# Two-term fp16 weights split from float32 in place, an output factor computed at a layer's start, and key norms by one squaring and one sum per half step

## The chip, the cores and the metric

The kernel runs on one core of a Trainium2 chip. A core has a matrix engine (TensorE, "PE" in the profile, with its weight loads as "PEld"), VectorE ("DVE"), ScalarE ("ACT"), GpSimd ("POOL"), SyncE ("SP", which issues the transfers here) and 16 DMA engines. Each engine takes its instructions strictly in order and waits on semaphores for the others. The metric is the device time of one execution in microseconds, the median of several.

## The reference

Delta-rule attention over 4 x 8 heads of 768 steps with head size 48, then two feed-forward layers over the 3072 tokens of width 384:

```python
k_n = k / (np.linalg.norm(k, axis=-1, keepdims=True) + 1e-06)
for t in range(S):
    kt, vt, bt = (k_n[:, :, t], v[:, :, t], beta[:, :, t, None])
    y[:, :, t] = np.einsum('bhd,bhde->bhe', q[:, :, t], state)
    v_old = np.einsum('bhde,bhd->bhe', state, kt)
    state = state + bt[:, :, :, None] * np.einsum('bhd,bhe->bhde', kt, vt - v_old)
...
h = x @ w_in          # first layer:  g = max(0.01 h, h)
g = ...               # second layer: g = h - tanh(h)
return g @ w_out      # d_model 384, d_ff 2048
```

All arrays are float32. The weights come in as 64-bit words (two 32-bit words for each number).

## The kernel before

**Numbers.** TensorE works on fp16. Each float32 operand is scaled by a power of two and split into a high fp16 part and a low one (value minus high part), and a product takes three matmuls: high by high, high by low, low by high.

**Work.** The 768 steps are cut into twelve chunks of 64 steps (n = 0 to 11), two to a unit u. For each chunk the attention makes normalised keys (`keys`, `key_scale`, `key_split`), Gram matrices (`grams`), products with q, states and outputs y (`outputs`). For each unit there is a triangular inverse (`inverses`): VectorE transposes `Gd` into `X`, GpSimd runs 30 steps of two tensor_tensor instructions each (`Gd<-X`, then `X<-X,Gd`), ScalarE and VectorE split the result (`Gd<-X`, `Gd<-X,Gd`), VectorE transposes it back, and merges on TensorE (`a_ps<-X,AT` and `a_ps<-XF,PM`) follow. y of a chunk is scaled and split by `to_xa` and `x_split` (ScalarE `xhi<-x,sxs`, then VectorE `x<-x,sxs,xhi`); that is the input of the first feed-forward layer.

**Layers.** `layer(n, i)` runs feed-forward layer i for chunk n, in the order (0,0), (1,0), (0,1), (1,1), (2,0) and so on: 24 passes, called pass 0 to pass 23 here. Each has eight parts p. `h_part` does 18 matmuls into `h_ps`, then ScalarE (and VectorE for i = 1) makes `sx`, and a high and a low `g`; `o_part` does the matmuls into the accumulators `o`, three parts behind. There is one pair of accumulators, so the first `o_part` of a pass waits until those of the pass before are copied out, for i = 1 by `osb<-o,kap` on ScalarE and on VectorE, one bank each.

**Weights.** Four weight tensors (0: w1_in in tile `wi_104`, 1: w1_out in `wo_106`, 2: w2_in in `wi_105`, 3: w2_out in `wo_107`) are loaded as word pairs. `w_f32` assembles float32 numbers in the destination itself with three VectorE instructions on 768 columns, ScalarE sums their squares, and `splits` turns each block of 384 columns into a high and a low fp16 half.

**Order.** The program runs a planner (`Plan`) while it is built: each instruction has an assumed cost, each engine an assumed clock, and side jobs (attention, weights) are put between the matmuls when they look ready. `tt` gives an elementwise instruction to VectorE or GpSimd, `cp` to VectorE or ScalarE, whichever the planner thinks ends first. All instructions of a scratch kind share one ring of four buffers (tag `sx`). A change of any instruction therefore reorders the program on every engine.

Nearly all instructions go through one line (L160), so the profile is read by tile names.

Of the kernel before, what the change touches and what calls it, by code (L numbers as in the profile page):

```python
# [191 lines left out]
def kernel(  # L192
# [18 lines left out]
    NG = 2  # L211
# [35 lines left out]
    def copy(o, i, scale=1.0):  # L247
        act.activation(out=o, in_=i, func=ACTF.Copy, scale=scale)
# [4 lines left out]
    def tt(o, a, b, op, lead=2.0):  # L253

        f = {e: plan.finish(e, "tensor_tensor", [a, b], [o]) for e in ("dve", "pool")}
        (dve if f["dve"] + lead < f["pool"] else pool).tensor_tensor(out=o, in0=a, in1=b, op=op)
# [85 lines left out]
    def at(*aps):  # L342
        return plan.at(*aps)
# [32 lines left out]
    class Weights:  # L376
# [36 lines left out]
            done.add((self.i, "s"))  # L413

        def splits(self):
            for f in range(NF):
                yield plan.t["act"]
                w = s_p.tile([128, DM], F32, tag="sx", name="wst")
                copy(w, self.f32[:, f], sw[:, self.i:self.i + 1])
                copy(self.dst[:, f, 0], w)  # L420
                tt(self.dst[:, f, 1], w, self.dst[:, f, 0], ALU.subtract, bias())
                done.add((self.i, f))

    def weights():
        wi = [words(w.rearrange("p f c n -> p (f c n)")) for w in WI2]
# [121 lines left out]
    def key_scale(a, y, t):  # L547

        dve.tensor_scalar(out=t, in0=a, scalar1=2.0 ** -100, scalar2=None, op0=ALU.max)
        dve.tensor_scalar(out=y.bitcast(I32), in0=t.bitcast(I32), scalar1=1, scalar2=POW2,  # L550
                          op0=ALU.logical_shift_right, op1=ALU.bitwise_and)
        dve.tensor_scalar(out=t, in0=y, scalar1=2.0 ** 64 / 0.85, scalar2=None, op0=ALU.mult)
        dve.reciprocal(out=y, in_=t)
        for it in range(5):
            if it in (1, 3):
                yield plan.t["dve"]
            dve.tensor_tensor(out=t, in0=y, in1=y, op=ALU.mult)
            dve.scalar_tensor_tensor(out=t, in0=t, scalar=-0.5, in1=a, op0=ALU.mult, op1=ALU.mult)
            dve.scalar_tensor_tensor(out=y, in0=t, scalar=1.5, in1=y, op0=ALU.add, op1=ALU.mult)
        dve.tensor_tensor(out=t, in0=a, in1=y, op=ALU.mult)  # L560
        dve.tensor_scalar(out=t, in0=t, scalar1=1e-6, scalar2=1.0 / KS, op0=ALU.add, op1=ALU.mult)
        dve.reciprocal(out=y, in_=t)
# [11 lines left out]
    def keys(n):  # L574

        yield from wait(("s", n - 4))
        load_k(n)
        kf = kf_t.pop(n)
        n2 = sm_p.tile([128, 3, NM], F32, tag="n2", name="n2", bufs=1)
        a, y, t = (n2[:, i] for i in range(3))  # L580
        for m in range(NM):
            if m % tune("k_m") == 0:
                yield max(plan.t["act"], at(kf))
            junk = s_p.tile([128, D], BF16, tag="junk", name="junk", bufs=1)
            square_sum(a[:, m:m + 1], kf[:, m], junk)
        yield max(plan.t["dve"], at(a))
        yield from key_scale(a, y, t)
        yield max(plan.t["act"], at(y))
        key_split(n, kf, y, tune("lead_k"))
# [376 lines left out]
    def h_part(i, x, p, kap):  # L966

        ps = ps_h.tile([128, 2 * N], F32, tag="h", name="h_ps")
        order = [(t, a, b) for t in range(KT) for a, b in ((0, 0), (0, 1), (1, 0))]
        if p == 0:  # L970
            order = [(t, a, 0) for t in range(KT) for a in range(2)] + [(t, 0, 1) for t in range(KT)]
        for j in range(2):
            for n, (t, a, b) in enumerate(order):
                mm(ps[:, j * N:(j + 1) * N], WI[i][:, 2 * p + j, a, t], x[b][:, t], n == 0, n == 3 * KT - 1)
                if n % tune("every") == tune("every") - 1:
                    side.step()
        sx = s_p.tile([128, 2 * N], F32, tag="sx", name="sx")
        if i == 0:
            act.activation(out=sx, in_=ps, func=ACTF.Prelu, scale=C0, alpha=0.01)
        else:  # L980
            act.activation(out=sx, in_=ps, func=ACTF.Tanh, scale=kap[:, 0:1])
            dve.scalar_tensor_tensor(out=sx, in0=sx, scalar=kap[:, 1:2], in1=ps, op0=ALU.mult, op1=ALU.add)
        g = g_p.tile([128, 2, 2 * N], F16, tag="g", name="g")
        if i == 0:
            copy(g[:, 0], sx)
            tt(g[:, 1], sx, g[:, 0], ALU.subtract, bias())
        else:
            split(g[:, 0], g[:, 1], sx, C0)
        return g

    def o_part(i, po, g, p):

        for j in range(2):
            f = 2 * p + j
            first, last = f == 0, f == NF - 1
            gj = g[:, :, j * N:(j + 1) * N]
            for o in range(KT if i == 0 else 2):
                if i == 0 and o == 0 and first:
                    mm(po[0], maskp[:, 0:1].to_broadcast([128, 128]), maskp[:, 0:1].to_broadcast([128, 512]), True, False)
                for n, (a, b) in enumerate(((0, 0), (0, 1), (1, 0))):  # L1000
                    if i == 0:
                        mm(po[o // 2][:, o % 2 * N:o % 2 * N + N], WO[0][:, f, a, o * 128:(o + 1) * 128], gj[:, b],
                           o == 2 and first and n == 0, o > 0 and last and n == 2)
                    else:
                        mm(po[o][:, 0:DM], gj[:, b, o * 128:(o + 1) * 128], WO[1][:, f, a], first and n == 0,
                           last and n == 2)
                side.step()

# [96 lines left out]
    def o_next():  # L1105
        n, i, p, g, kap, sx, po = pend.pop(0)
        if p == 0:
            po += [ps_o.tile([128, 512], F32, tag=f"o{o}", name=f"o{o}") for o in range(2)]
        need((2 * i + 1, 2 * p + 1))
        side.step(plan.at(g, WO[i][:, 2 * p], WO[i][:, 2 * p + 1]))  # L1110
        o_part(i, po, g, p)
        if p < NP - 1:
            return
        if i == 0:
            gen = to_xb(n, po, sx)
            e = side.add(gen, "xb")
            side.advance(e)
            return
        out_scale(kap)
        for o in range(2):  # L1120
            ob = s_p.tile([128, DM], F32, tag="sx", name="osb")
            if o % 2:
                dve.tensor_scalar(out=ob, in0=po[o][:, 0:DM], scalar1=kap[:, 2:3], scalar2=None, op0=ALU.mult)
            else:
                copy(ob, po[o][:, 0:DM], kap[:, 2:3])
            for h in range(2):
                r0 = (2 * o + h) * S + n * C
                sp.dma_start(out=out[r0:r0 + C], in_=ob[h * C:(h + 1) * C])

    def layer(n, i):  # L1130
# [8 lines left out]
        else:  # L1139
# [5 lines left out]
            x, sx = xb_t.pop(n)  # L1145
            need((2, "s"))
            kap = kappa(sx)
        po = []
        for p in range(NP):
            need((2 * i, 2 * p + 1))  # L1150
# [84 lines left out]
```

## Time and profile before

| what | value |
|---|---|
| median of 3 runs | 1221.16 us (1218.24 to 1222.01) |
| profiled execution | 1222.18 us, span 1220.3 us, mean granted clock 0.97 |
| TensorE busy | 1013.1 us, 83% of the span |
| VectorE, ScalarE, GpSimd busy | 736.5, 634.0 and 509.1 us |
| read from and written to memory | 41.09 MB and 4.72 MB |

Shares are over the whole span. A row of a timeline begins with its start in microseconds from the span's start and its length; a bracket at its end is the idle time of the engine ahead of it, and what ended that. A group row gives the count, the busy time, the mean of one in ns, and after the second bar the idle time ahead of them.

### The profile page before, as it was taken

The page shows a single profiled execution, that of the slowest core. Times are in us where ns is not written, and L with a number is a line of the kernel's source. Part 1 is how long each engine was busy: PE and PEld are TensorE (multiplying, and loading weights), DVE is VectorE, ACT ScalarE, POOL GpSimd, SP SyncE. Part 2 cuts the span into 40 slices and gives each one's busy share as a digit, 9 for nine tenths or more (in the row PEclk, how much of TensorE's full clock was granted, in tenths as well). Part 3 has the DMA queues.
Part 4 walks back from the last instruction along what each step waited for, and adds up shares of the span by engine and source line. Part 5 has one row for each costly group of instructions (what it writes and reads, how often), then busy time and mean ns, then how long its engine had stood idle before and what let it go on. Part 6 is the DMA issues. An engine that isn't in the chain of part 4 may idle for free.

```text
span 1220.3 us, 36850 instructions
## 1 busy us (share of the span) xinstructions
PE 1013.1 (83%) x16216; PEld 831.8 (68%) x16216; DVE 736.5 (60%) x1592; ACT 634.0 (52%) x1409; POOL 509.1 (42%) x635
## 2 busy tenths in 40 slices
PE   0301658898798989989999888899999999999998
PEld 0201547686686878857787766678867888778875
DVE  7997896857567567777755665546753064420243
ACT  3555679695356655645567534435543364333332
POOL 4597446388214872483332682485110321012100
PEclk9999999899898989989999898999999999999999
DMA  9423133100001000000111000001000000000001
GB/s 363 154 84 113 55 106 96 37 24 1 16 23 39 24 22 17 26 23 24 39 32 37 24 1 16 10 8 33 25 10 14 14 12 2 11 17 1 1 1 27
DMA packets 21857, 48.17 MB, mean 39 GB/s; under 512 B 4288, under 2 KB 7360, under 8 KB 21696
## 3 DMA queue, kind: packets, MB, share of 16 engines
q1 hardware_dynamic: 21696, 45.82, 11.9%
q8 instruction: 126, 2.06, 0.7%
q14 instruction: 35, 0.29, 0.1%
HBM read 41.09 MB, written 4.72 MB: 38 GB/s over the span
## 4 chain that ended last, share of the span: by engine, by line
PE 51%; DVE 26%; ACT 11%; POOL 8%; issue 4%; DMA 0%; ACTq 0%; SPq 0%; DVEq 0%; POOLq 0%
PE o L160 21%; PE h_ps L160 19%; PE a_ps L160 11%; DVE n L160 4%; POOL X L160 3%; POOL Gd L160 3%; DVE x L160 2%; ACT g L160 2%; DVE wi L160 2%; DVE g L160 2%; DVE sx L160 2%; DVE wo L160 2%; ACT junk L160 1%; ACT sx L160 1%; DVE X L160 1%
## 5 line engine op out<-in xcount | busy, mean ns | idle before, releaser
L160 PE MATMUL h_ps<-x,wi 128*128 128x256 f16 x3456 | 427.9, 276 | 18.3 <-DVE x L160 12.3
L160 PEld LDWEIGHTS <-wi 128*128 128x128 f16 x3456 | 336.5, 99 | 77.6 <-issue 23.6
L160 PE MATMUL o<-wo,g 128*128 128x384 f16 x1152 | 214.9, 337 | 25.5 <-ACT osb L160 16.0
L160 POOL TENSOR_TENSOR g<-sx,g 128x512 f16<-128x512 f32 x78 | 93.1, 1194 | 311.6 <-ACT g L160 291.6
L160 PE MATMUL o<-g,wo 128*128 128x256 f16 x1728 | 210.6, 275 | 0.0
L160 PEld LDWEIGHTS <-wo 128*128 128x128 f16 x1728 | 167.4, 98 | 32.3 <-issue 10.5
L160 ACT ACTIVATE g<-sx 128x512 f16<-128x512 f32 x192 | 121.0, 630 | 120.2 <-DVE sx L160 117.2
L160 PEld LDWEIGHTS <-g 128*128 128x128 f16 x1152 | 113.7, 100 | 96.0 <-issue 36.0
L160 DVE SCALAR_TENSOR_TENSOR sx<-sx,kap,h_ps 128x512 f32<-128x512 f32 x96 | 71.2, 741 | 92.9 <-ACT sx L160 92.6
L160 POOL TENSOR_TENSOR Gd<-X 128x30 f32<-128x30 f32 (+9 forms) x180 | 110.8, 616 | 33.3 <-DVE X L160 19.5
L160 POOL TENSOR_TENSOR X<-X,Gd 128x30 f32<-128x30 f32 (+9 forms) x180 | 114.8, 638 | 14.1
L160 DVE SCALAR_TENSOR_TENSOR g<-sx,g 128x512 f16<-128x512 f32 x96 | 74.3, 774 | 67.4 <-ACT g L160 67.4
L160 ACT ACTIVATE sx<-h_ps,kap 128x512 f32<-128x512 f32 x96 | 65.4, 681 | 81.6 <-PE h_ps L160 71.3
L160 ACT ACTIVATE sx<-h_ps 128x512 f32<-128x512 f32 x96 | 56.5, 589 | 93.9 <-PE h_ps L160 87.6
L160 PEld LDWEIGHTS <-KTp 64*64 64x64 f16 x3360 | 66.2, 118 | 36.4 <-issue 34.4
L160 POOL TENSOR_TENSOR P<-P,maskp 128x1024 f16<-128x1024 f16 x24 | 52.6, 2196 | 61.4 <-DVE P L160 58.2
L160 PE MATMUL a_ps<-ab,ones 128*128 128x1 bf16 x124 | 11.7, 168 | 75.3 <-DVE ab L160 73.4
L160 PEld LDWEIGHTS <-KN 64*64 64x64 f16 x1824 | 37.5, 120 | 39.7 <-issue 35.7
L160 PE MATMUL a_ps<-Q,Sb 128*128 128x64 f16 x528 | 35.7, 199 | 13.2 <-DVE Sb L160 13.2
L160 PEld LDWEIGHTS <-ones 128*128 128x128 bf16 x124 | 7.8, 102 | 54.0 <-DVE ab L160 50.0
L160 PE MATMUL a_ps<-Q,KTp 64*64 64x64 f16 x1152 | 25.4, 201 | 23.1 <-ACT Q L160 20.2
L160 ACT ACTIVATE x<-a_ps,qs 32x128 f32<-32x128 f32 (+1 forms) x57 | 25.5, 447 | 31.4 <-PE a_ps L160 28.2
(161 smaller groups left out, 1533.1 us busy)
## 6 DMA issues: line engine op xcount, KB each, us to landing
wo<-in_w_in_dram SPq DMA_DIRECT2D x32, 384.0 KB, 6.1
qf<-in_q_dram SPq DMA_DIRECT2D x24, 256.0 KB, 2.6
wi<-in_w_out_dram SPq DMA_DIRECT2D x14, 384.0 KB, 7.8
kf<-in_k_dram SPq DMA_DIRECT2D x12, 384.0 KB, 4.1
vf<-in_v_dram SPq DMA_DIRECT2D x12, 384.0 KB, 4.1
out_dram<-osb SPq DMA_DIRECT2D x48, 96.0 KB, 2.2
wo<-in_w_out_dram SPq DMA_DIRECT2D x8, 384.0 KB, 3.8
stage<-in_w_out_dram SPq DMA_DIRECT2D x8, 384.0 KB, 3.8
```

What stands on the lines that cost most here:

```text
L160: return getattr(self.eng[eng], op)(*args, **kw)
```

## The change

Three edits, and what the planner makes of them.

`splits` takes two blocks at a time. ScalarE writes the scaled fp16 high half of 768 columns into a scratch tile `wh`, VectorE writes the low half from the float32 numbers over their own place (`lo_of`), and a transfer on SyncE's queue copies `wh` into the other half. The halves of a weight change places, hence `1 - a` where they are read. In `keys`, eight heads are squared at once and VectorE sums them; in `key_scale` an integer first guess and three refinements stand in place of a reciprocal and five. `out_scale`, three small VectorE instructions, goes from the end of a pass with i = 1 to its start.

```diff
         def splits(self):
-            for f in range(NF):
+            s_ = sw[:, self.i:self.i + 1]
+            for f in range(0, NF, 2):
                 yield plan.t["act"]
-                w = s_p.tile([128, DM], F32, tag="sx", name="wst")
-                copy(w, self.f32[:, f], sw[:, self.i:self.i + 1])
-                copy(self.dst[:, f, 0], w)
-                tt(self.dst[:, f, 1], w, self.dst[:, f, 0], ALU.subtract, bias())
-                done.add((self.i, f))
+                w = s_p.tile([128, 2, DM], F16, tag="sx", name="wh")
+                copy(w, self.f32[:, f:f + 2], s_)
+                lo_of(self.dst[:, f:f + 2, 0], self.f32[:, f:f + 2], s_, w)
+                sp.dma_start(out=self.dst[:, f:f + 2, 1], in_=w)
+                done.update((self.i, f + i) for i in range(2))
...
     def key_scale(a, y, t):
-        dve.tensor_scalar(out=y.bitcast(I32), in0=t.bitcast(I32), scalar1=1, scalar2=POW2,
-                          op0=ALU.logical_shift_right, op1=ALU.bitwise_and)
-        dve.tensor_scalar(out=t, in0=y, scalar1=2.0 ** 64 / 0.85, scalar2=None, op0=ALU.mult)
-        dve.reciprocal(out=y, in_=t)
-        for it in range(5):
-            if it in (1, 3):
+        dve.tensor_scalar(out=t.bitcast(I32), in0=t.bitcast(I32), scalar1=1, scalar2=None,
+                          op0=ALU.logical_shift_right)
+        dve.tensor_scalar(out=y.bitcast(I32), in0=t.bitcast(I32), scalar1=-1.0, scalar2=float(0x5F375A00),
+                          op0=ALU.mult, op1=ALU.add)
+        for it in range(3):
+            if it == 1:
...
-        for m in range(NM):
-            if m % tune("k_m") == 0:
-                yield max(plan.t["act"], at(kf))
-            junk = s_p.tile([128, D], BF16, tag="junk", name="junk", bufs=1)
-            square_sum(a[:, m:m + 1], kf[:, m], junk)
+        for g in range(NG):
+            gs = slice(g * GM, (g + 1) * GM)
+            yield max(plan.t["act"], at(kf))
+            qs = s_p.tile([128, GM, D], F32, tag="sx", name="ksq")
+            act.activation(out=qs, in_=kf[:, gs], func=ACTF.Square)
+            dve.tensor_reduce(out=a[:, gs], in_=qs, axis=AX.X, op=ALU.add)
...
-        out_scale(kap)
         for o in range(2):
             ob = s_p.tile([128, DM], F32, tag="sx", name="osb")
...
             need((2, "s"))
             kap = kappa(sx)
+            out_scale(kap)
```

Over the whole program VectorE goes from 1593 to 1547 instructions, ScalarE from 1157 to 923 activations, GpSimd from 639 to 594, SyncE's transfers rise by 32, and TensorE keeps its 16216 matmuls.

On GpSimd, inside the first inverse (steps 15 and 16 of its 30), the difference reads:

```order
 L160 TENSOR_TENSOR Gd<-X 128x16x15
 L160 TENSOR_TENSOR X<-X,Gd 128x16x15
-L160 TENSOR_TENSOR wi_104<-wst,wi_104 128x384
 L160 TENSOR_TENSOR Gd<-X 128x15x16
 L160 TENSOR_TENSOR X<-X,Gd 128x15x16
```

Four such splits of w1_in stood among the steps of the first inverse, and none stands there now; the second inverse had six of w2_out and has none.

On VectorE, behind the input of pass 0 (`x<-x,sxs,xhi` is the low half of that input), what follows before is the last of the word assembly (from `stage`) and attention work:

```order
L160 SCALAR_TENSOR_TENSOR x<-x,sxs,xhi 128x768
L160 COPY x<-xhi 128x768
L160 SCALAR_TENSOR_TENSOR wo_107<-stage,wo_107 128x768
L160 SCALAR_TENSOR_TENSOR Gd<-a_ps,maskb,Gd 128x256
L160 SCALAR_TENSOR_TENSOR AT<-a_ps,half,AT 128x256
```

In the changed program the assembly of w2_out only begins there, among the splits of w2_in and the norms of keys (`n_1757`):

```order
L160 SCALAR_TENSOR_TENSOR wo_107<-wo_107 128x768
L160 TENSOR_SCALAR wo_107<-wo_107 128x768
L160 SCALAR_TENSOR_TENSOR wo_107<-wo_107 128x768 x2
L160 SCALAR_TENSOR_TENSOR wi_105<-wi_105,sw,wh 128x2x384
L160 TENSOR_TENSOR n_1757<-n_1757 128x16
L160 SCALAR_TENSOR_TENSOR n_1757<-n_1757 128x16 x2
```

Between the low half of pass 0's input and that of pass 1's stand 88 instructions before and 140 now. The 52 more are 9 scalar_tensor_tensor and 5 tensor_scalar of word assembly, 8 splits, 17 small key instructions, 3 sums, 3 key scalings, 3 key splits, a transpose of `Gd` and some ten instructions on one column, less some copies.

At the first end of a pass with i = 1 VectorE had, before:

```order
L160 SCALAR_TENSOR_TENSOR g<-sx,g 128x512
L160 TENSOR_SCALAR kap<-sw 128x1
L160 RECIPROCAL kap<-kap 128x1
L160 TENSOR_TENSOR kap<-kap 128x1
L160 TENSOR_SCALAR osb<-o_4335,kap 128x384
```

and now:

```order
L160 SCALAR_TENSOR_TENSOR sx<-sx,kap,h_ps 128x512
L160 SCALAR_TENSOR_TENSOR g<-sx,g 128x512
L160 TENSOR_SCALAR osb<-o_4348,kap 128x384
L160 SCALAR_TENSOR_TENSOR x<-x,sxs,xhi 128x768
L160 COPY x<-xhi 128x768
```

The three instructions on `kap` are gone from that place; they follow the six of `kappa` at the pass's start.

## Rows read from the trace of the kernel before

**Rows 1.** The page: busy time by engine.

```profile
PE 1013.1 (83%) x16216; PEld 831.8 (68%) x16216; DVE 736.5 (60%) x1592; ACT 634.0 (52%) x1409; POOL 509.1 (42%) x635
```

**Rows 2.** Windows: length, then busy PE, PEld, DVE, ACT, POOL; clock, DMA share, GB/s.

```profile
113.00:181.70 68.70, 35.97 (x1138) 34.05 (x1138) 64.10 (x110) 49.63 (x116) 32.50 (x29) 1.00 0.31 105
181.70:235.00 53.30, 43.81 (x598) 37.13 (x598) 40.65 (x89) 42.54 (x104) 25.61 (x23) 0.97 0.24 75
235.00:381.40 146.40, 133.82 (x2313) 107.14 (x2313) 92.34 (x214) 88.37 (x217) 71.39 (x98) 0.93 0.07 19
381.40:943.00 561.60, 515.56 (x9125) 420.77 (x9125) 356.60 (x816) 291.91 (x677) 261.45 (x349) 0.96 0.08 22
943.00:1220.30 277.30, 270.55 (x2641) 220.71 (x2638) 89.51 (x199) 107.35 (x179) 40.03 (x33) 1.00 0.04 9
```

**Rows 3.** Chain of waits, first inverse's first and last step; GpSimd's group of splits, 50 to 110.

```profile
50.00 0.85 POOL Gd L160
...
109.68 0.33 POOL X L160
...
L160 POOL TENSOR_TENSOR wi<-wst,wi 128x384 f16<-128x384 f32 x4 | 5.3, 1332 | 0.0
```

**Rows 4.** VectorE's timeline: split of the first inverse, inputs of pass 0 and pass 1.

```profile
111.41 1.54 DVE L160 TENSOR_TENSOR Gd<-X,Gd 128x1024 f16<-128x1024 f32 x1 [4.91 <-ACT Gd L160]
...
179.65 1.01 DVE L160 SCALAR_TENSOR_TENSOR x<-x,sxs,xhi 128x768 f16<-128x768 f32 x1
...
233.54 1.01 DVE L160 SCALAR_TENSOR_TENSOR x<-x,sxs,xhi 128x768 f16<-128x768 f32 x1
```

**Rows 5.** TensorE's timeline: first matmuls of pass 0 and of pass 1.

```profile
181.70 5.79 PE L160 MATMUL h_ps<-x,wi 128*128 128x256 f16 x27 [5.57 <-DVE x L160]
...
235.00 2.50 PE L160 MATMUL h_ps<-x,wi 128*128 128x256 f16 x11 [3.86 <-DVE x L160]
```

**Rows 6.** VectorE's groups: two of word assembly (the second from 181.7 to 235), key instructions.

```profile
L160 DVE SCALAR_TENSOR_TENSOR wi<-wo,wi 128x768 int32<-128x768 int32 x32 | 34.3, 1071 | 0.7
...
L160 DVE SCALAR_TENSOR_TENSOR wo<-stage,wo 128x768 int32<-128x768 int32 x7 | 11.5, 1642 | 0.2
...
L160 DVE SCALAR_TENSOR_TENSOR n<-n 128x16 f32<-128x16 f32 x100 | 30.7, 307 | 3.4
```

**Rows 7.** ScalarE's groups: key squares, their accumulator reads, high half of x.

```profile
L160 ACT ACTIVATE junk<-kf 128x48 bf16<-128x48 f32 x160 | 37.9, 237 | 2.7
L160 ACT ACTIVATION_READ_ACCUMULATOR junk<-kf 128x1 f32 x160 | 30.1, 188 | 0.0
L160 ACT ACTIVATE xhi<-x,sxs 128x768 f16<-128x768 f32 x24 | 22.2, 924 | 4.9 <-DVE sxs L160 3.0 <-DVE ab L160 1.7 <-DVE n L160 0.2
```

**Rows 8.** GpSimd's timeline, second inverse: first and last instruction, one split; two GpSimd groups.

```profile
261.45 0.25 POOL L160 TENSOR_TENSOR Gd<-X 128x30 f32<-128x30 f32 x1 [1.07 <-DVE X L160]
264.39 0.91 POOL L160 TENSOR_TENSOR wo<-wst,wo 128x384 f16<-128x384 f32 x1
313.61 0.64 POOL L160 TENSOR_SCALAR X<-bt 128x32 f32<-128x32 f32 x1
...
L160 POOL TENSOR_TENSOR g<-sx,g 128x512 f16<-128x512 f32 x78 | 93.1, 1194 | 311.6 <-ACT g L160 291.6 <-issue 17.6 <-DVE p L160 1.3
L160 POOL TENSOR_TENSOR P<-P,maskp 128x1024 f16<-128x1024 f16 x24 | 52.6, 2196 | 61.4 <-DVE P L160 58.2 <-DVE n L160 1.9 <-DVE p L160 1.3
```

**Rows 9.** TensorE's waits from 235 on: in total, times, longest; the end of pass 2.

```profile
PE o L160 <- ACT osb L160: 19.6, 8, 5.9
...
325.41 0.58 ACT L160 ACTIVATE osb<-o,kap 128x384 f32<-128x384 f32 x1 [1.28 <-DVE kap L160]
326.05 0.65 PE L160 MATMUL o<-wo,g 128*128 128x384 f16 x3 [4.15 <-ACT osb L160]
```

**Rows 10.** One kind of transfer: count, size of one, median us from issue to landing.

```profile
qf<-in_q_dram SPq DMA_DIRECT2D x24, 256.0 KB, 2.6
```

More of the change, by code (lines that the diff above doesn't have):

```diff
@@ L973, in h_part @@
             for n, (t, a, b) in enumerate(order):
-                mm(ps[:, j * N:(j + 1) * N], WI[i][:, 2 * p + j, a, t], x[b][:, t], n == 0, n == 3 * KT - 1)
+                mm(ps[:, j * N:(j + 1) * N], WI[i][:, 2 * p + j, 1 - a, t], x[b][:, t], n == 0, n == 3 * KT - 1)
                 if n % tune("every") == tune("every") - 1:
@@ L1001, in o_part @@
                     if i == 0:
-                        mm(po[o // 2][:, o % 2 * N:o % 2 * N + N], WO[0][:, f, a, o * 128:(o + 1) * 128], gj[:, b],
+                        mm(po[o // 2][:, o % 2 * N:o % 2 * N + N], WO[0][:, f, 1 - a, o * 128:(o + 1) * 128], gj[:, b],
                            o == 2 and first and n == 0, o > 0 and last and n == 2)
                     else:
-                        mm(po[o][:, 0:DM], gj[:, b, o * 128:(o + 1) * 128], WO[1][:, f, a], first and n == 0,
+                        mm(po[o][:, 0:DM], gj[:, b, o * 128:(o + 1) * 128], WO[1][:, f, 1 - a], first and n == 0,
                            last and n == 2)
```

## The prediction

> **What bounds the kernel now.** I read the page first, for the busy times [rows 1]: TensorE is busy for 83% of the span, so 207 us of it are gaps, and the question is where they lie. The windows answer that [rows 2]. From 943 us to the end TensorE is busy for 270.55 of 277.3 us. From 381 to 943 it is busy for 92%, from 235 to 381 for 91%, from 181.7 to 235 for 82%, and ahead of 181.7 hardly at all. So the first 235 us hold most of what can be won, and work taken from the other engines after 943 us is worth nothing.
>
> The chain of waits shows who holds the start: from 50.00 to 110.01 us it runs through GpSimd, from the first to the last step of the first triangular inverse [rows 3]. Then VectorE takes over. It splits the inverse at 111.41 and writes the last input of pass 0 at 179.65 [rows 4], and in the window from 113 to 181.7, nearly the same stretch, it is busy for 64.10 of 68.70 us [rows 2]. TensorE starts pass 0 at 181.70 and pass 1 at 235.00, both times after an idle stretch that ended with VectorE's `x`, of 5.57 and 3.86 us [rows 5]. In the 53.3 us between, TensorE has 43.81 us of work and VectorE 40.65 [rows 2]. From 235 on TensorE's largest wait that the change touches is for `osb`, 19.6 us in 8 places [rows 9].
>
> The profiled execution took 1222.18 us, 1.0 above the median shown. The sum is made against it, and the median's worth is taken off at the end. A measurement of this kernel can tell 0.3%, 3.7 us, from no change.
>
> **The first inverse: -0.9 and -6.2 us.** (a) Seven of `key_scale`'s small VectorE instructions go, at 307 ns [rows 6] 2.1 us. A product that now stands on VectorE and a sum take about half of it back, so GpSimd starts the inverse some 0.9 earlier (bounds 0 and -2.1). (b) Four splits of w1_in leave the inverse itself, 5.3 us of the 60.0 [rows 3]. It ends near 103.8 instead of 110.01 if nothing takes their place. The cost of a lesser gain is the rival on contention, below.
>
> **VectorE from the inverse to pass 0: -5.9 us.** (c) In the order, the work between the split of the inverse and the last input of pass 0 changes thus: word assembly falls from 28 instructions to 22, seven splits and three sums come, seven small key instructions go. Priced by 1.07 us for assembly [rows 6], 1.01 for a split (the low half of x has the same form and 768 columns [rows 4]), 0.31 for a small one and 0.5 for a sum, with the rest of the small changes, that is -2.9 on the path. Then GpSimd is busy beside it for 32.50 us [rows 2], nearly all in splits that go, and two-input VectorE instructions run long in such a place: the seven on 768 columns between 181.7 and 235 took 1.64 us each where the mean of the other 32 is 1.07 [rows 6]. I take 3 back from this, from bounds of 0 and 5. Pass 0 then starts at 181.7 - 0.9 - 5.3 - 5.9 = 169.6.
>
> **VectorE from pass 0 to pass 1: it becomes the bound.** (d) Here the change puts work back. 140 instructions stand between the two inputs where 88 stood. Nine of assembly at 1.07 are 9.6 us, eight splits at 1.01 are 8.1, 17 key instructions at 0.31 are 5.3 [rows 4, 6]. A tensor_scalar on 768 columns lies between 0.31 and 1.07; five at 0.6 are 3.0. Three sums on 384 columns at 0.5, six key scalings and splits at 0.73, one transpose at 2 and ten one-column ones at 0.16 are estimates between the same rows, together 9.5. Against these 35.5 some seven instructions leave, at 0.9 about 6. That is +29; 4 come off because the seven at 1.64 would run at 1.07. VectorE's 40.65 becomes 65.5, and with 5 us of idle time where the window before had 12.65, the stretch lasts 70.5. Pass 1 starts at 169.6 + 70.5 = 240.1, **5.1 us later** than the 235.00 of before, although pass 0 starts 12 earlier. TensorE's 43.81 us of pass 0 [rows 2] do not cover that: it idles some 20 us ahead of pass 1, since both orders place all of pass 0's `o` matmuls ahead of pass 1's first. The prices' ends (0.31 or 1.07 for what has no row, idle 0 to 9) give -3 to +14.
>
> **The second inverse: +3 us.** (e) It lasts 52.8 us before, 261.45 to 314.25, and holds six splits at 0.91 [rows 8]; without these 47.3. The new order puts four `g` products at 1.19 and two `P` masks at 2.2 [rows 8] into it: 56.5. What waits for it (VectorE's split, then the merges on TensorE) stood in pass 3 and stands in pass 2 now, a window of about 50 us. It can be some 6 us late, and VectorE, in order, would hold the `g` and `sx` of pass 2 behind its split. TensorE has parts of that pass queued, so I take half: +3, from 0 to +10.
>
> **The output's factor: -6.5 us.** (f) At the first end of a pass with i = 1 ScalarE's copy waits 1.28 us for `kap`, and TensorE 4.15 for that copy [rows 9]. With the factor made in the pass's start the 1.28 goes, and the copies themselves (0.58) and their queue stay. At each of the longer waits I take 1.35, at the short ones what they hold: -6.5 of 19.6 (bounds -4 and -9). The three instructions now stand behind `kappa`, where VectorE has slack.
>
> **Relief of ScalarE: -6 us.** (g) 160 squares at 237 ns with reads at 188 are 68.0 us [rows 7]; twenty squares on 384 columns at about 0.5 replace them. From 235 to 943 ScalarE is busy for 380 of 708 us [rows 2], and loses some 55, a seventh. TensorE's gaps in that stretch are 58.6 us; those for `osb` are counted already, and a seventh of the rest is 6. Nothing excludes 0, nor 10.
>
> **At no cost.** The 32 new transfers of 192 KB: one of 256 KB lands in 2.6 us [rows 10], and in the order the last split that a pass needs stands 16 VectorE rows and more ahead of the pass's input, 10 us or more. Without that cover each would add its 2.6 to the first `o` of a pass. SP's queue is in order, so a load of later words now waits behind a copy that waits for its split; DMA is busy for 24 to 31% then [rows 2], so the loads have room, but a ring slot of `sx` stays held until its copy has landed. The new high half costs ScalarE one 768-column instruction of 0.924 [rows 7] in place of four of half the width; ScalarE doesn't set the end of the startup. The refinement's sums and fewer steps in later chunks lie beside TensorE's work.
>
> **Sum.** +5.1 + 3 - 6.5 - 6 = -4.4 us after the start; (a) to (c) are inside the +5.1. 1222.2 - 4.4 = 1217.8, or 1217 on the median shown.
>
> **Rivals.** *VectorE's stretch is no bound* (faster). If assembly and splits run at their quiet prices and the idle time vanishes, the stretch is 62 us instead of 70.5, pass 1 starts near 231.6, and with the full relief of 10 the time is 1217 - 8.5 - 4 = 1204. For it: the seven at 1.64 show how much of a price is GpSimd's neighbourhood. Against it: 140 instructions in order with transposes and products from TensorE between them, which gave 12.65 us of idle time before.
>
> *VectorE's stretch is the bound at the upper prices* (slower). Mechanism (d) alone, from pass 0's `x` to pass 1's: 79 us, pass 1 at 249, +14 instead of +5.1, gives 1226. It decides from about 75 us on, where nothing that follows can pay for it. For it: VectorE is already busy for 93% of the stretch ahead of it [rows 2], and assembly has nowhere else to go. Against it: GpSimd, the neighbour that slows it, loses work.
>
> *The inverses don't get shorter* (no change). The first inverse takes 54.7 us without its splits, the second 47.3 without its own [rows 3, 8], though both have 30 steps: VectorE's busy neighbourhood costs the first 7.4. The splits that leave GpSimd run on VectorE, on two tensors, beside the same inverse. If they slow it by what they cost there, the 5.3 stay, pass 0 and pass 1 come 5 later, and the time is 1222. The Trainium skill ("GPSIMD Engine Reference", section "1. Specifications") says that GpSimd's SBUF interfaces are shared with VectorE, with contention where a VectorE instruction has two SBUF inputs; by it this rival's mechanism is real, and the 54.7 against 47.3 agrees, though no run here has separated the two yet.
>
> **How the numbers follow.** Forecast 0.42, faster rival 0.20, slower rival 0.24, contention 0.14. The forecast's own range is 1208 to 1223, from the bounds of (d) to (g) taken together, not all at one end. The range of 8 in 10 goes from 1203, just below the faster rival, to 1232, the slower rival with half of (e)'s upper bound on top. The bound of 0.3% puts "same" at 1217.5 to 1224.8. Of the forecast about half lies below, of the faster rival nearly all, of contention a tenth: faster 0.44. Above lie a tenth of the forecast, most of the slower rival and a fifth of contention: slower 0.30; same 0.26.
>
> **What would show it.** (b) right: GpSimd's first inverse ends near 104; still 59 us long, and contention is right. (c) right: pass 0 starts near 170. (d) right: 65 us or more of VectorE work between the two inputs, pass 1's first matmul at 237 to 243 behind an idle stretch of TensorE of 15 to 25 us; at 232 the faster rival, at 249 the slower. (e) right: VectorE's split of the second inverse waits for GpSimd in pass 2. (f) right: no `osb` waits for `kap`, and the waits for `osb` sum to about 13 us. (g) right: from pass 1 to the last quarter TensorE's stretch shortens by more than (f) gives. Wrong altogether it would be if the new order delayed a later unit's states or a transfer of a weight, neither of which I price.

## The result, and the profile after

The changed kernel takes 1230.8 us (median), the kernel before 1221.6: a ratio of 1.0079, interval 1.0067 to 1.0092. It is **slower by 9 us** where 1217, 4 us faster, was forecast; the value lies inside the range of 1203 to 1232, near its upper end. The profiled execution took 1232.5 us, its span is 1230.7.

The page's busy times, beside [rows 1]: ScalarE and GpSimd lost what the change takes off them, VectorE's total stayed.

```profile
PE 1008.6 (82%) x16216; PEld 829.8 (67%) x16216; DVE 737.2 (60%) x1546; ACT 561.7 (46%) x1015; POOL 471.0 (38%) x590
```

The windows of the changed kernel, cut at its own pass 0, pass 1 and pass 16 (length, busy PE, PEld, DVE, ACT, POOL, clock, DMA share, GB/s):

```profile
0.00:170.51 170.51, 47.05 (x1542) 44.05 (x1543) 145.22 (x250) 73.76 (x139) 87.64 (x111) 0.62 0.47 161
170.51:246.45 75.94, 46.49 (x742) 39.71 (x742) 67.89 (x141) 44.08 (x85) 31.72 (x35) 0.81 0.33 107
246.45:954.84 708.39, 645.01 (x11294) 525.32 (x11294) 435.22 (x961) 336.42 (x614) 311.61 (x412) 0.95 0.08 23
954.84:1230.70 275.86, 270.06 (x2640) 220.74 (x2638) 88.88 (x196) 107.39 (x179) 40.03 (x33) 1.00 0.04 9
```

Against [rows 2]: pass 0 starts 11.2 us earlier (170.51 for 181.70), the stretch to pass 1 is 75.94 us instead of 53.30, so that pass 1 starts 11.5 later, and the 708 us behind it did not get shorter. The last 276 us are nearly as before (277). So the stretch between pass 0 and pass 1 loses 22.6 us, twice what the start had won, and nothing is won back behind it, where I had counted 9.5.

GpSimd's timeline, first and last step of the first inverse, then of the second [rows 3, 8]:

```profile
49.07 0.84 POOL L160 TENSOR_TENSOR Gd<-X 128x30 f32<-128x30 f32 x1 [2.82 <-DVE X L160]
...
104.91 0.32 POOL L160 TENSOR_SCALAR X<-bt 128x32 f32<-128x32 f32 x1
...
233.95 0.28 POOL L160 TENSOR_TENSOR Gd<-X 128x30 f32<-128x30 f32 x1 [12.64 <-DVE n L160]
...
294.89 0.64 POOL L160 TENSOR_SCALAR X<-bt 128x32 f32<-128x32 f32 x1
```

The first lasts 56.2 us (60.0 before), the second 61.6 (52.8), and the second begins 27 us earlier. VectorE between the two inputs [rows 4, 6], from its timeline:

```profile
169.06 1.01 DVE L160 SCALAR_TENSOR_TENSOR x<-x,sxs,xhi 128x768 f16<-128x768 f32 x1
...
231.86 2.01 DVE L160 STREAM_TRANSPOSE X<-Gd 128x1024 f32<-128x1024 f32 x1
...
239.57 1.24 DVE L160 SCALAR_TENSOR_TENSOR wo<-stage,wo 128x768 int32<-128x768 int32 x1
240.74 0.87 DVE L160 TENSOR_TENSOR KN<-kn,KN 128x384 f16<-128x384 f32 x1
241.53 0.86 DVE L160 TENSOR_TENSOR kn<-kf,n 128x384 f32<-128x384 f32 x1
...
244.62 1.06 DVE L160 SCALAR_TENSOR_TENSOR x<-x,sxs,xhi 128x768 f16<-128x768 f32 x1 [0.17 <-ACT xhi L160]
```

and TensorE meanwhile [rows 5]:

```profile
236.82 0.25 PE L160 MATMUL a_ps<-ab,ones 128*128 128x1 bf16 x2 [10.39 <-DVE ab L160]
246.45 0.80 PE L160 MATMUL h_ps<-x,wi 128*128 128x256 f16 x3 [9.38 <-DVE x L160]
```

VectorE transposes the second unit, assembles w2_out and makes keys while TensorE idles for 10.4 and 9.4 us. Behind that, TensorE's waits (from 246.45 to 954.8: in total, times, longest) beside [rows 9]:

```profile
PE h_ps L160 <- DVE x L160: 21.4, 3, 10.0
...
PE o L160 <- ACT osb L160: 8.4, 3, 4.0
...
PE h_ps L160 <- DVE sx L160: 6.2, 3, 3.1
```

The wait for `osb` fell from 19.6 to 9.1 (8.4 for ScalarE's copy and 0.7 for VectorE's), more than forecast. In its place stands, ahead of pass 7, this (SyncE's queue, ScalarE, VectorE and TensorE, from the timeline):

```profile
576.83 0.43 SPq L160 DMA_DIRECT2D kf<-in_k_dram  x1
...
580.03 0.94 ACT L160 ACTIVATE ksq<-kf 128x384 f32<-128x384 f32 x2 [4.55 <-DMA kf<-in_k_dram]
580.59 1.01 DVE L160 TENSOR_REDUCE n<-ksq 128x8 f32<-128x384 f32 x2 [1.52 <-ACT ksq L160]
...
581.83 1.23 DVE L160 SCALAR_TENSOR_TENSOR x<-x,sxs,xhi 128x768 f16<-128x768 f32 x1 [0.23 <-ACT xhi L160]
...
583.67 5.40 PE L160 MATMUL h_ps<-x,wi 128*128 128x256 f16 x36 [9.97 <-DVE x L160]
```

A load of keys was issued 3 us ahead of its use; ScalarE stood 4.55 us behind it, in order, with the high half of pass 7's input queued next, and TensorE stood 9.97 us.

### The profile page after: what moved, and what is told of

It reads as the page before. It is cut to its first block, busy times and chain, and to the rows that moved or that the text cites. A ratio compares the mean times of both kernels' runs of the same rounds, so it can differ in the third digit from the quotient of the medians.

```text
span 1230.7 us, 36497 instructions
## 1 busy us (share of the span) xinstructions
PE 1008.6 (82%) x16216; PEld 829.8 (67%) x16216; DVE 737.2 (60%) x1546; ACT 561.7 (46%) x1015; POOL 471.0 (38%) x590
## 3 DMA queue, kind: packets, MB, share of 16 engines
q1 hardware_dynamic: 30400, 52.11, 13.4%
## 4 chain that ended last, share of the span: by engine, by line
PE 42%; DVE 4%; POOL 3%; ACT 2%; issue 1%; POOLq 0%; ACTq 0%; DVEq 0%
PE o L160 19%; PE h_ps L160 18%; PE a_ps L160 5%; POOL X L160 2%; POOL Gd L160 1%; DVE n L160 1%; DVE x L160 1%; DVE Ub L160 0%; DVE Sb L160 0%; DVE sx L160 0%; DVE g L160 0%; ACT xhi L160 0%; DVE kap L160 0%; ACT g L160 0%; DVE p L160 0%
## 5 line engine op out<-in xcount | busy, mean ns | idle before, releaser
L160 PE MATMUL h_ps<-x,wi 128*128 128x256 f16 x3456 | 432.9, 279 | 33.9 <-DVE x L160 22.0
L160 POOL TENSOR_TENSOR g<-sx,g 128x512 f16<-128x512 f32 x82 | 97.4, 1189 | 338.6 <-ACT g L160 325.4
L160 PE MATMUL o<-g,wo 128*128 128x256 f16 x1728 | 215.0, 277 | 0.8 <-issue 0.8
L160 PE MATMUL o<-wo,g 128*128 128x384 f16 x1152 | 206.0, 328 | 4.8 <-ACT x L160 3.0
L160 DVE SCALAR_TENSOR_TENSOR sx<-sx,kap,h_ps 128x512 f32<-128x512 f32 x96 | 71.4, 744 | 104.0 <-ACT sx L160 103.8
L160 POOL TENSOR_TENSOR X<-X,Gd 128x30 f32<-128x30 f32 (+9 forms) x180 | 118.7, 659 | 14.1
L160 DVE COPY Ub<-R 64x768 f16<-64x768 f16 x46 | 26.1, 567 | 70.5 <-PE a_ps L160 69.9
L160 PEld LDWEIGHTS <-ones 128*128 128x128 bf16 x124 | 8.0, 105 | 75.4 <-issue 42.9
L160 POOL TENSOR_TENSOR Gd<-Gd,tri 128x256 f32<-128x256 f32 x24 | 18.7, 780 | 74.3 <-DVE Gd L160 74.2
```

The source lines that it names most:

```text
L160: return getattr(self.eng[eng], op)(*args, **kw)
```

## The experiments

Two theories stood at first. **A**: the edits themselves cost the 9 us, by what they give VectorE to do ahead of pass 1. **B**: the loss lies in the order that the planner dealt anew, not in the edits. In the tables "p1" is pass 1's first matmul and "idle" TensorE's idle time from there to pass 16's first, both in the profiled execution (235.0 and 58.6 us in the kernel before, 246.5 and 63.4 in the changed one). The ratio is to the kernel before, timed on the same chip.

**The edits one by one.** e1 is the kernel before with the hunk of `splits` (and its `1 - a`), e2 with that of `out_scale`, e3 with those of `keys` and `key_scale`; e5 is the changed kernel without those two.

```diff
 e1: -copy(w, self.f32[:, f], ...); copy(self.dst[:, f, 0], w); tt(self.dst[:, f, 1], ...)
     +copy(w, self.f32[:, f:f + 2], s_); lo_of(...); sp.dma_start(out=self.dst[:, f:f + 2, 1], in_=w)
 e2:  kap = kappa(sx)
     +out_scale(kap)
 e3: -square_sum(a[:, m:m + 1], kf[:, m], junk)
     +act.activation(out=qs, in_=kf[:, gs], func=ACTF.Square); dve.tensor_reduce(out=a[:, gs], ...)
 e5: the change without the lines of e3
```

> The kernel before with the edit of the splits alone. Theory A (the splits give VectorE, which bounds the start, more to do between the inputs of pass 0 and pass 1 than GpSimd's relief takes off ahead of pass 0): pass 0 starts at 167 to 174, pass 1 at 243 to 250, and the time is 1226 to 1234, most of the +9.2. Theory B (any edit deals the planner's order anew, and the stalls of the middle, such as the one of 10 us ahead of pass 7, decide): pass 1 late too, but the total can lie anywhere from 1212 to 1236, and the gaps of TensorE after pass 1 differ from those of both kernels by 5 us or more.

> The kernel before with the output's factor made at the start of the pass, and nothing else. Theory A: pass 1 stays at 235, the waits for osb fall from 19.6 to 8 to 13, and the time falls by 5 to 11 (1210 to 1216). Theory B: the waits fall alike, but the new order of the middle gives it back: 1217 to 1226.

> The kernel before with the edit of the key norms alone. Theory A (the key norms matter little, since ScalarE has slack): pass 1 at 232 to 240, time within 4 of before (1217 to 1226). A rival, theory C: two squares on 384 columns on ScalarE, in order behind a load of keys that comes late, hold up what is queued behind them, as ahead of pass 7 in the changed kernel; then the time is 5 or more above before (over 1226) and TensorE shows a gap of over 5 us behind such a wait.

> The changed kernel without its edit of the key norms (splits and factor stay). Ahead of pass 1 it has the same order as the run of the splits alone. Theory A (what VectorE has to do ahead of pass 1's input sets the loss): pass 1 at 237 to 240 again, and the factor takes 2 to 8 off behind it: 1225 to 1232. Theory B (each deal of the order has its own stalls): pass 1 at 238 too, but the stretch behind it is not within 6 us of the 987 of the splits alone.

| run | us | ratio (interval) | p1 | idle |
|---|---|---|---|---|
| e1 | 1233.6 | 1.0097 (1.0082 to 1.0111) | 238.5 | 64.5 |
| e2 | 1219.5 | 0.9973 (0.9951 to 0.9996) | 234.6 | 58.6 |
| e3 | 1248.1 | 1.0215 (1.0200 to 1.0230) | 265.6 | 59.9 |
| e5 | 1221.2 | 0.9975 (0.9953 to 0.9997) | 238.9 | 55.7 |

The parts do not add up: +12.5, -1.6 and +27 against +9.2 for all. Splits and factor together (e5) give -1.5, not +11. The keys, for which the forecast had -0.9 in (a), -6 in (g) and part of the work in (d), cost 27 alone. In e3 the loss stands in the start (pass 0 at 196.0, pass 1 at 265.6), and ScalarE's squares wait for 2.1 us in all, none of it for a load of keys: theory C (a late load of keys) has the time but not the place. Theory A has the time of e1 but not its pass 1, which comes only 3.5 us later than before where 8 to 15 were expected; and e5 has the same order ahead of pass 1, the same p1 and 12 us less, below A's range. In e2 the time is B's, not A's.

**VectorE's work moved away from pass 1.** e4 holds w2_out's assembly until pass 1's input is written (and makes the factor at the pass's first `o_part`, since it needs w2_out's scale), e6 the key norms; e7 splits the second layer's weights in the old way, e8 is e7 without the edit of the keys.

```diff
 e4:  b = Weights(3, w2_out, WO[1], r)
     +yield from wait(("n", 1))
      yield from b.convert()
 e6:  yield from wait("w1")
     +yield from wait(("n", 1))
      yield from keys(n)
 e7: +if self.i > 1: (the three old lines for each f)
```

> The changed kernel, with the assembly of w2_out held until the low half of pass 1's input is written, and the output's factor made three parts into the pass rather than at its start. Theory A: VectorE has some 15 us less to do between the two inputs, pass 1 starts at 228 to 236 instead of 246, and w2_out, needed from pass 2 on, is ready in time or up to 5 us late: 1217 to 1225. Theory B: pass 1 as early, but the 10 us are given back in the middle: 1226 to 1234. If w2_out comes late as a whole, TensorE waits for its split in pass 2 by 10 us or more, and the time is 1228 or more.

> The changed kernel, with the key norms of chunk 2 and later held until the low half of pass 1's input is written; no work is left out. Theory A: VectorE sheds some 27 us of key norms, key products and the second transpose ahead of pass 1, which starts at 226 to 234 instead of 246; the second inverse starts some 15 to 25 us later than 234, about where it started before the change (261), so the gain stays: 1214 to 1223. Rival D (the order of VectorE's work is a zero sum, as holding w2_out showed): pass 1 as early, but chunk 2's states and so pass 4 come late by as much, 1228 to 1240.

> The changed kernel, with the two weights of the second layer split as before the change (scaled float32 copies on ScalarE, low halves on whichever of VectorE and GpSimd is thought to end first). Theory A: GpSimd is busy for only 16 of 66 and 32 of 76 us in the two stretches ahead of pass 1 and has room; VectorE sheds eight splits (some 9 us) ahead of pass 1 and eight behind pass 2: pass 1 at 236 to 241, time 1219 to 1227. Theory B: no better than 1228.

> The kernel of the run before this one, without the edit of the key norms as well: new splits for the first layer's weights alone, and the early factor. Theory A: VectorE's work ahead of pass 1's input is back at what it was before the change, while the first inverse keeps its 4 us: pass 1 at 228 to 235, time 1210 to 1219, ahead of both kernels. Theory B or D: 1220 or more.

| run | us | ratio (interval) | p1 | idle |
|---|---|---|---|---|
| e4 | 1241.5 | 1.0153 (1.0134 to 1.0172) | 229.6 | 76.4 |
| e6 | 1232.7 | 1.0084 (1.0063 to 1.0106) | 216.3 | 80.2 |
| e7 | 1247.7 | 1.0200 (1.0181 to 1.0219) | 244.5 | 73.2 |
| e8 | 1218.6 | 0.9962 (0.9947 to 0.9977) | 230.0 | 66.3 |

Theory A hits with e8, and with pass 1 but not the time of e4; its times for e4, e6 and e7 are too low by 10 us or more. Rival D has the time of e6, but not the place: pass 4 starts at 386 us there, not later than the changed kernel's 396. In e4 TensorE also waits 6.1 us in pass 2 for the copy of a late split of w2_out, a transfer that the forecast had at no cost as long as it was covered.

Pass 1 can be had 30 us earlier than in the changed kernel, and the time stays (e6). Its windows, ahead of pass 0, to pass 1, and to pass 16:

```profile
0.00:160.50 160.50, 43.02 (x1381) 40.20 (x1382) 136.01 (x224) 67.77 (x126) 80.58 (x103) 0.62 0.49 165
160.50:216.30 55.80, 41.41 (x487) 34.84 (x486) 45.75 (x89) 35.39 (x66) 15.01 (x9) 0.90 0.39 121
216.30:954.00 737.70, 657.44 (x11707) 535.47 (x11708) 463.40 (x1036) 355.03 (x652) 328.29 (x440) 0.94 0.09 25
```

The stretch behind pass 1 is 29 us longer than the changed kernel's: it holds 413 more matmuls, for 12 us more of TensorE's work, and 17 us more of gaps. So a late pass 1 is not the cause by itself, and theory A in its simple form falls.

**The pace of the keys.** A third theory, E: two cheap squares let the keys of later chunks run ahead, and the VectorE work that they bring ahead of pass 3 decides. e9 puts the sixteen squares back, e10 paces the keys of chunk n by the input of pass n - 3, e12 is e7 with the sixteen squares.

```diff
 e9: -act.activation(out=qs, in_=kf[:, gs], func=ACTF.Square); dve.tensor_reduce(...)
     +square_sum(a[:, m:m + 1], kf[:, m], junk)
 e10: yield from wait("w1")
     +yield from wait(("n", max(n - 3, 0)))
      yield from keys(n)
```

> The changed kernel with the squares of the keys as before (sixteen on ScalarE, one for each head, with their sums), and the shorter refinement kept. Theory E (the harm is in the two cheap squares: they let the key norms of later chunks pass the planner's gate on ScalarE early, and so put key norms, key products and the second unit's merges on VectorE ahead of pass 1 and pass 3, at the cost of the inputs of these passes): VectorE's work ahead of the input of pass 3 falls by some 40 us against the changed kernel, and the time is 1216 to 1225, as without the whole edit of the keys. Rival F (the shorter refinement, or any new order with it, costs it): 1227 to 1235.

> The changed kernel with all its edits, with the key norms of chunk n held until the input of pass n - 3 of the first layer is written (chunk 2 and 3: that of chunk 0; chunk 4: that of chunk 1; and so on). Nothing is left out. Theory E: the order ahead of pass 3 holds as much VectorE work as without the edit of the keys, pass 1 starts at 233 to 241, and the time is 1216 to 1225. Rival F: the pace of the keys is not it, 1227 to 1236; the run that held all keys until pass 1 gave 1232.7, since it made the second unit late.

> The changed kernel with new splits for the first layer's weights alone, the squares of the keys as before, the shorter refinement and the early factor. Theory E: the lowest VectorE work ahead of pass 1 of all the kernels with the shorter first inverse; pass 1 at 227 to 234 and 1209 to 1219. Theory B: anywhere from 1212 to 1240.

e9 gave 1224.3 (1.0041, 1.0028 to 1.0055), e10 1218.6 (0.9978, 0.9961 to 0.9994), as E has it (though e10's pass 1 came at 229.5, ahead of its 233 to 241); e12 gave 1238.4 (1.0144, 1.0130 to 1.0158) and missed by 19 us, with p1 at 228.7. What follows shows why neither hit nor miss counts for much.

**The order alone.** The planner's assumed delay between engines is moved from 0.15 us to 0.14 or 0.16: no instruction changes, only where some stand. e11 and e15 do this to the changed kernel, e13 and e14 to the one before, e16 to e10.

```diff
-    GAP = 0.15
+    GAP = 0.16
```

> The changed kernel, with one assumed number of the planner moved by a little (the delay between engines, 0.15 to 0.16 us), which changes no instruction but where some stand. A measure of theory B: if any new order moves the time by 5 us or more, the result is below 1226 or above 1236; if the loss belongs to the edits, it is 1227 to 1235.

> The kernel before with the planner's delay between engines at 0.14 us instead of 0.15: same instructions, another order. Priced by the durations of the traces, VectorE has 216 us of work ahead of the fourth input of a layer, 222 in the kernel before, 279 in the changed one. Theory E (that work sets the loss): 1216 to 1225. Theory B (each order has its own luck, worth 5 us or more either way, whatever the edits): outside of 1216 to 1226.

> The kernel before with the planner's delay at 0.16 us: 220 us of VectorE work ahead of the fourth input. Theory E: 1216 to 1225. Theory B: outside of 1216 to 1226.

> The changed kernel with the planner's delay at 0.14 us: 286 us of VectorE work ahead of the fourth input, 279 in the changed kernel. Theory E: it stays slow, 1229 to 1250. Theory B: it can be as fast as before, 1215 to 1250.

> The changed kernel with paced keys (1218.6 with 236 us of VectorE work ahead of the fourth input) and the planner's delay at 0.14 us, by which that work rises to 270 though the keys are paced as they were. Theory E: slow again, 1229 to 1245. Rival F (the pace of the keys as such, or the edits as such): 1214 to 1224.

| kernel | 0.14 | 0.15 | 0.16 | mean ratio |
|---|---|---|---|---|
| before | 1245.4 (1.0180) | 1221.6 | 1241.6 (1.0151) | 1.011 |
| changed | 1223.9 (1.0012) | 1230.8 (1.0079) | 1244.9 (1.0198) | 1.010 |
| e10 | 1252.1 (1.0237) | 1218.6 (0.9978) | not run | |

The same instructions in three orders differ by 24 us before the change and by 21 after it, far more than the 9.2. The order of the kernel before was the best of its three. Over three orders each the two kernels have the same mean, but with such a spread three orders cannot tell a difference of some 10 us or less (an estimate from the ratios in the table). Theory E falls with e13, which has the least VectorE work of all ahead of pass 3's input and takes 1245 us, and with e15, which has more of it than the changed kernel and takes 7 us less. The loss shows behind pass 1, in e13's and e14's windows from there to pass 16, which hold the same 11436 or so matmuls as the 708.00 us of the kernel before (58.6 us idle there, 77.3 and 75.4 here):

```profile
237.70:966.00 728.30, 651.00 (x11436) 534.38 (x11436) 446.18 (x1020) 386.21 (x899) 334.80 (x446) 0.94 0.07 20
```

```profile
237.40:962.00 724.60, 649.21 (x11436) 529.69 (x11436) 454.45 (x1025) 381.43 (x890) 337.15 (x452) 0.94 0.08 21
```

Gaps are not all of it. e11 has the changed kernel's instructions, and behind its pass 1 the same 11294 matmuls; that stretch is 7.6 us longer than the changed kernel's 708.39, with 1.3 us more of gaps and 6.3 more of busy time (651.36 for 645.01), at a granted clock of 0.94 for 0.95:

```profile
251.00:967.00 716.00, 651.36 (x11294) 529.64 (x11294) 438.62 (x956) 332.80 (x608) 316.81 (x411) 0.94 0.08 22
```

What does belong to the edits in all three orders is the start: pass 0 at 170.5, 169.4 and 167.6 against 181.7, 179.7 and 179.0, and pass 1 at 246 to 251 against 235 to 238.

**The edits in the order of before.** The planner counts the old instructions without issuing them, and the new ones are issued in their places: TensorE's order is the kernel before's to the last row, and the other engines differ only where an edit adds, drops or replaces an instruction. e17 has all three edits, e18 the factor alone. The piece for the splits; the squares, the refinement and `out_scale` are treated alike:

```diff
-copy(w, ...); copy(self.dst[:, f, 0], w); tt(self.dst[:, f, 1], ...)
+(the same three, counted by the planner and not issued)
+if f % 2:
+    E["act"].activation(out=wh, in_=self.f32[:, fs], func=ACTF.Copy, scale=s_)
+    E["dve"].scalar_tensor_tensor(out=self.dst[:, fs, 0], ...)
+    E["sp"].dma_start(out=self.dst[:, fs, 1], in_=wh)
```

> All three edits, put into the order of the kernel before: the planner counts the old instructions, and the new ones are issued in their places, so that TensorE's order is that of before to the last row, and VectorE, ScalarE, GpSimd and SyncE differ only where an edit adds, drops or replaces an instruction. Theory A (the edits themselves cost the 9 us, by VectorE's work ahead of pass 1): 1226 to 1236. Theory B (the loss is that of the order that the edits dealt; by themselves they win the terms on the first inverse, on the factor and on ScalarE): 1206 to 1218, pass 0 at 172 to 179, pass 1 at 229 to 237.

> The factor edit alone, in the order of the kernel before: three VectorE instructions move from each end of a pass to its start and nothing else moves on any engine. The size of the term on the factor: with the waits for osb falling from 19.6 to about 13, 1213 to 1217; 1219 to 1223 if a later wait takes the gain up.

e17 takes **1204.3 us**, a ratio of 0.9848 (0.9831 to 0.9865), 18.7 below the kernel before and 26 below the changed one: the version that beats both. e18 takes 1217.2 (0.9951, 0.9938 to 0.9965), just above its range. Theory A is out. B's range was 2 us too high, its pass 1 is right, and its pass 0 (172 to 179) is not: the win is not in the start. e17's windows, cut at pass 0, pass 1 and pass 16:

```profile
0.00:183.49 183.49, 47.80 (x1542) 44.71 (x1543) 153.91 (x274) 75.87 (x143) 80.02 (x104) 0.61 0.48 165
183.49:232.95 49.46, 41.08 (x597) 35.27 (x597) 38.27 (x90) 32.88 (x60) 16.77 (x13) 0.95 0.32 97
232.95:927.37 694.42, 644.39 (x11439) 524.56 (x11439) 454.29 (x993) 343.64 (x633) 327.05 (x436) 0.96 0.09 24
927.37:1203.20 275.83, 270.06 (x2640) 220.72 (x2638) 88.86 (x196) 107.40 (x179) 40.05 (x33) 0.99 0.04 9
```

Against [rows 2], pass 0 starts 1.8 us later, pass 1 2.1 earlier, and 13.6 are won from pass 1 to pass 16 with the same matmuls: TensorE idles 50.0 us there instead of 58.6, and the matmuls themselves take 5.0 less (the granted clock is 0.96 for 0.95). The last quarter gives 1.4 more. Two rows of TensorE's waits from 160 to 960, beside [rows 9]:

```profile
PE o L165 <- ACT osb L165: 9.4, 4, 4.7
...
PE o L165 <- DVE osb L165: 3.1, 2, 1.8
```

The start is instructive. GpSimd ends the first inverse at 105.6 instead of 110.0, but VectorE, in order, comes to its split only at 109.6 (111.4 before). From there to pass 0's input (182.0) VectorE has twelve splits of 768 columns where the kernel before had one of 384. It is busy for 64.67 us, hardly more than the 63.67 of before, since assembly and key instructions got cheaper; but it waits 3 us for ScalarE's high halves (`wst`), and the stretch is 4.2 us longer. The kernel before and e17, from the split to the input (what the clock's 1.00 in the first is worth, the last section says):

```profile
111.41:179.65 68.24, 35.97 (x1138) 34.05 (x1138) 63.67 (x108) 49.64 (x113) 31.75 (x29) 1.00 0.34 110
```

```profile
109.60:182.00 72.40, 34.88 (x1138) 33.11 (x1138) 64.67 (x114) 34.47 (x64) 6.48 (x6) 0.52 0.40 129
```

VectorE's groups there, in the kernel before:

```profile
L160 DVE SCALAR_TENSOR_TENSOR wi<-wo,wi 128x768 int32<-128x768 int32 x10 | 11.5, 1155 | 0.2
L160 DVE SCALAR_TENSOR_TENSOR wo<-wo 128x768 int32<-128x768 int32 x8 | 10.0, 1248 | 0.2
L160 DVE TENSOR_SCALAR wi<-wo 128x768 int32<-128x768 int32 x4 | 4.3, 1087 | 0.0
```

and in e17:

```profile
L165 DVE SCALAR_TENSOR_TENSOR wi<-wo,wi 128x768 int32<-128x768 int32 x10 | 9.8, 980 | 0.2
L165 DVE SCALAR_TENSOR_TENSOR wo<-wo 128x768 int32<-128x768 int32 x8 | 8.2, 1022 | 0.2
L437 DVE SCALAR_TENSOR_TENSOR wi<-wi,sw,wst 128x768 f16<-128x768 f32 x7 | 7.1, 1014 | 3.1 <-ACT wst L436 3.1
...
L165 DVE TENSOR_SCALAR wi<-wo 128x768 int32<-128x768 int32 x5 | 2.8, 551 | 0.0
```

GpSimd's busy time beside them fell from 31.75 to 6.48 us, and the instructions on 768 columns run 15 to 50% shorter.

## Why the prediction was wrong

**The step that failed is the sum itself**: it takes the new order's cost to be what it does to VectorE ahead of pass 1, and sets against it 9.5 us of terms behind pass 1, as if the other stalls there stayed those of the old order. It has -4.4 where the profiled spans show +10.4. Of this miss of 15 us, 6.4 lie at pass 1 (+11.5 for +5.1) and 8.5 behind it (-1.0 for -9.5). Behind pass 1 every new order sets its own stalls: TensorE is idle there for 57 to 77 us in the three orders of either kernel, and e13 and e14, without any edit, lose 20 and 17 us there. I had priced none of this but the second inverse. "Wrong altogether it would be if the new order delayed a later unit's states or a transfer" names this at the end, without a chance or a price. No rival was an order as such.

**Terms of the start.** (a) with (b): the inverse ended at 105.2 against a forecast of 103.8; it starts 0.9 earlier, as said, and lasts 56.2 instead of 54.7. The 5.3 us gave 3.8 here and 2.6 in e17, so the contention rival's mechanism took back up to half of it, not all. (c): pass 0 at 170.5, forecast 169.6, so (c) came out right (-6.4 for -5.9); but the pieces that it lists add up to about nothing, and its -2.9 rests on "the rest of the small changes", which it does not show. (d): the stretch from pass 0 to pass 1 is 75.9 us, forecast 70.5; VectorE is busy for 67.9 (65.5) and idle for 8 (5). TensorE waits 19.8 us at the end of pass 0, as forecast. The size was off by 5, between forecast and slower rival, and that rival's place and mechanism are in the trace; e1 with e5, and e6, show that it does not decide the time by itself.

**Terms behind pass 1**, forecast -9.5, in the dealt order -1.0 (+11.5 at pass 1, +10.4 by the spans, unrounded). (f), forecast -6.5: e18, where nothing else moves, gave -5.8 (-4.3 to -7.6), and `osb` waits of 13.4 us, as forecast. So the waits and the size were right, but the waits did not turn into time as the sum has it. e18 from pass 1 to pass 16, to be set beside the 708.00 us of before (649.38 busy, 58.6 idle, clock 0.95):

```profile
234.77:936.50 701.73, 641.75 (x11438) 522.85 (x11438) 454.54 (x1032) 380.11 (x893) 334.54 (x447) 0.97 0.08 21
```

TensorE is idle for 60.0 us there, no less than before, since other waits grew by as much; what fell is the busy time of the same 11438 matmuls, by 7.6 us, at a higher granted clock. In the kernel before the clock stands at 0.50 (1.2 GHz) from 538.8 to 545.6 and from 791.4 to 794.8 us, at two of its long `osb` waits (5.2 and 3.3 us); in e18 the waits at these places are below 2 us each, and the clock is 1.00 there. That shorter waits gave the higher clock is what these two profiles suggest; no run separates it. In the dealt order 10.5 us of `osb` waits went and the stall ahead of pass 7 alone took 10 back. (e): the second inverse lasts 61.6, forecast 56.5, but began 27 us earlier, so nothing waited for its length. The copies on SyncE's queue, costed at nothing, land in 2.3 to 2.4 us, and TensorE has no wait for one in the changed kernel or in e17 (one of 6.1 us in e4). (g), forecast -6: e17 less e18 leaves -12.9 for splits and keys in a held order (9.2 between the two profiled spans, 1.8 of them by pass 1), so there is relief behind pass 1, of the forecast's size, and it is idle time that falls (60.0 to 50.0 us). Which of the two edits brings it, and whether by ScalarE's relief, was not separated.

**Contention.** The Trainium skill ("GPSIMD Engine Reference", section "1. Specifications") says that GpSimd's SBUF interfaces are shared with VectorE, with contention where a VectorE instruction has two SBUF inputs or runs in a 2-port mode. The measured groups agree: with GpSimd quiet the assembly's two-input instructions fell from 1155 to 980 ns, its one-input tensor_scalar from 1087 to 551. Within the trace of the kernel before it is the same: of the 32 `wi<-wo,wi` the 14 with hardly any GpSimd instruction beside them take 0.93 to 0.96 us, the nine wholly beside one 1.14 on average. Whether tensor_scalar runs in a 2-port mode here no trace shows. I had taken 3 us for contention in (c); in e17 it is part of what lets twelve splits go into that stretch for 1 us of VectorE's busy time.

**What stays open**: which property of an order makes it slow, and how much of that is the granted clock. VectorE's work ahead of pass 3 is not it (e13, e15), nor p1 (e6). And e17's gain is shown in one order, a good one.

## What to carry to other kernels

Where a planner sets the order from assumed costs, any edit is two changes, itself and a new deal of the order. Measure the second by moving a cost that alters no instruction, before believing a difference: here that alone moved the time by 24 us. To time an edit, or to keep its gain, hold the order and put the edited instructions into it; three edits that measured +9 us are worth -19 that way. And compare TensorE's busy time as well as its gaps: for the same 11438 matmuls behind pass 1 it went from 641.75 us (e18) to 651.4 (e13).

## What the runs showed that was not expected

A granted clock can be read wrongly. In the profile of before it is 1.00 for the whole startup [rows 2], in that of the changed kernel 0.62 from 0 to 170.5, as if one had run at 2.4 GHz and the other at 1.2 for most of it. e18 has the order of the kernel before, and so the same matmuls; the kernel before and e18 from 113 to 175 us:

```profile
113.00:175.00 62.00, 34.83 (x1105) 32.95 (x1106) 57.50 (x104) 43.49 (x101) 28.86 (x26) 1.00 0.35 115
```

```profile
113.00:175.00 62.00, 34.88 (x1105) 33.00 (x1106) 57.50 (x104) 43.52 (x101) 28.83 (x26) 0.50 0.35 116
```

The same 1105 matmuls take the same time where the clock reads 1.00 and where it reads 0.50, and the 192 of `a_ps<-R,XF` take 224 ns each in both; matmuls of that form and size take 187 ns on average in the kernel before from 240 to 900 us. So TensorE ran alike in the two, and the 1.00 of before is no measurement: that trace has no record of the clock ahead of 187 us, where e18's begins at 36, and a stretch without a record reads 1.00. The mean of 0.97 of that execution is too high by it; runs of the kernel before with a mean of 0.91 and of 0.97 lie mixed between 1217 and 1226 us. The clocks behind pass 1, on which the readings above rest, are on record in every trace.
